# Block-diagonal inverses, 64-row update steps and a hold on small steps in a delta-rule recurrence with a gated MLP

## The chip, the cores and the metric

The kernel runs on one core of a Trainium2 chip. A core has a tensor engine (PE, with a sequencer of its own for weight loads, PEld in the profile), a vector engine (VectorE, DVE), a scalar engine (ScalarE, ACT), GpSimd (POOL) and SyncE (SP), which starts most transfers. The metric is the device time of one execution in microseconds (us). Before the change the median of three runs is 633.71 us (633.09 to 634.2).

## The reference

```python
# q, k, v: (B, H, S, D) = (4, 8, 768, 48); beta: (4, 8, 768); all f32
k_n = k / (norm(k, axis=-1) + 1e-06)
state = zeros((B, H, D, D))
for t in range(S):
    y[:, :, t] = einsum('bhd,bhde->bhe', q[:, :, t], state)
    v_old = einsum('bhde,bhd->bhe', state, k_n[:, :, t])
    state += beta[:, :, t, None, None] * einsum('bhd,bhe->bhde', k_n[:, :, t], v[:, :, t] - v_old)
x = y.transpose(0, 2, 1, 3).reshape(3072, 384)
out = (sigmoid(x @ w_gate) * (x @ w_val)) @ w_out      # w_gate, w_val 384 x 1536, w_out 1536 x 384
```

So 32 independent recurrences (4 batches by 8 heads) of 768 tokens each, and a gated MLP on the result.

## The kernel before

**Groups.** The 768 tokens are cut into 12 groups g of 64 tokens. Inside a group the recurrence is solved in closed form for all 32 heads together. The Gram matrix of the keys gives a lower triangular 64x64 system for each head, cut into two halves of 32 tokens: two 32x32 diagonal blocks and a 32x32 corner under them. VectorE inverts the diagonal blocks, for two groups (a pair) at once, one row of the solution after the other; the transposed inverses of a pair lie in `mt`. Tiles have 128 partitions, four quarters of 32: a head's 64 tokens fill one half of the partitions, and of the 32 heads half lie in partitions 0-63 and half in 64-127. `e` says whether a head's two token halves stand in order (0) or swapped (1), `x` in which half of the partitions (together with e) they stand, `j` counts the 8 heads of each of the four kinds (e, x).

**The steps of a group on PE**, each of many small f32 matmuls on parts of the 128x128 array, four in turn on different parts: `pg` (Gram, `gram`, L254); `pp` (keys by queries, `masked`, L273, then masked on VectorE); `pk` (keys by state, `rest`, L384); the first solution `pu` (step 0 of `updates`, L414, inverse by R = v - pk); its product with the corner (step 1, L407, added into pk); the second solution (step 2, L414 again); `yy` (outputs, `rows`, L442 and L445); `pd` (the change of the state, `advance`, L469); and the transposes `pt` (`flip`, L500), which give the x of the MLP. Between them VectorE subtracts (`less`, L393) and updates the state `su` (L478), and ScalarE copies solutions out of PSUM (`keep_u`, L422) and outputs (`keep_y`). Groups 0 and 1 start the program: they invert only 16x16 blocks and join them by two products, `pz` and `pm` (`joining`, L366), which `lower_left` feeds.

**The MLP.** Groups 0 and 1 form a unit each (tiles 256 tokens wide), then two groups a unit (512 wide). A gate or value tile (`gate_val`, L521, lines `gv_g` and `gv_v`) has 9 matmuls, 3 slices of the model's width by 3 products of values split into two parts; an output tile (`outp`, L557, `po`) has 9 too. Before the first gate tile PE fills gaps with dummy matmuls, `warm` (L185).

**The order.** `schedule()` plans every engine's order when the program is built: each step is a task with a cost in ns, what it comes after and which buffers it takes and frees (`pools`); a table `URGENCY` shifts tasks. Engines then run their queues in that fixed order, with semaphores between them. Transfers go through SyncE's queue: per group `dk` and `dq` (keys and queries by dimension, into `kqp`), `dv` (v and beta) and `dt` (k rows, for pd).

## Time and profile before

| what | value |
|---|---|
| median of 3 runs | 633.71 us (633.09 to 634.2) |
| the profiled execution | 636.26 us, of it 634.5 us span of the core |
| mean TensorE clock granted | 0.991 |
| PE busy | 617.0 us, 97% of the span, 9372 records |
| weight loads (PEld) | 502.4 us, 79% |
| VectorE | 393.7 us, 62% |
| ScalarE | 255.9 us, 40% |
| GpSimd | 10.0 us, 2% |
| largest groups | po 167.5, gv_g 167.3, gv_v 136.9 us on PE |

In a row of a group stand line, engine, operation, out<-in, for PE rows the place on the array (rows*columns) and the moving operand, the number of records, then busy us and mean ns of one, then the idle time before it and what ended most of it. In a row of stretches stand the stretch, its length, and the busy time (records) of PE, PEld, DVE, ACT and POOL, the granted clock, the share of the DMA engines and GB/s. In a row of the timeline stand start and length in us, and records in a run of like instructions. A row of waits has the waiting group, the releaser, then us in all, how often, and the longest.

### The profile page before, as it was taken

The numbers are of one execution on the slowest core, as the hardware profiler recorded it, in microseconds if no ns is written. First come the engines' busy times: TensorE is split into PE (matmuls) and PEld (weight loads), VectorE is DVE, ScalarE is ACT, GpSimd is POOL, SyncE is SP. The second block draws the span as 40 slices with busy tenths as digits, with TensorE's granted clock in tenths as the row PEclk, the third lists the DMA queues.
The fourth block names the chain that finished last, engine by engine and source line by source line (L and its number), as shares of the span: only waits on it lengthen the run. The fifth ranks groups of instructions, "written<-read, shape, count | busy, mean of one in ns | idle before, by whom it ended". The sixth has DMA issues, their size and how long they took to land.

```text
span 634.5 us, 20716 instructions
## 1 busy us (share of the span) xinstructions
PE 617.0 (97%) x9372; PEld 502.4 (79%) x9381; DVE 393.7 (62%) x876; ACT 255.9 (40%) x506; POOL 10.0 (2%) x25
## 2 busy tenths in 40 slices
PE   8878999999999999999999999999999999999997
...
GB/s 220 263 167 219 190 189 96 2 28 113 61 50 26 27 110 38 2 74 5 23 112 28 35 101 2 26 66 48 35 101 1 1 3 3 2 51 0 1 1 50
DMA packets 16216, 40.75 MB, mean 64 GB/s; under 512 B 2944, under 2 KB 3968, under 8 KB 16128
## 3 DMA queue, kind: packets, MB, share of 16 engines
...
## 4 chain that ended last, share of the span: by engine, by line
PE 87%; ACT 5%; DVE 5%; issue 1%; DMA 1%; SPq 0%; ACTq 0%
PE gv_g L521 26%; PE po L557 22%; PE gv_v L521 20%; PE pu L414 3%; PE warm L185 3%; PE pk L384 2%; PE pp L273 2%; PE yy L442 2%; PE pg L254 2%; PE yy L445 2%; ACT G L258 1%; PE pd L469 1%; PE pt L500 1%; PE pk L407 1%; ACT w L172 1%
## 5 line engine op out<-in xcount | busy, mean ns | idle before, releaser
L521 PE MATMUL gv_g<-x,w 128*128 128x512 f32 (+1 forms) x756 | 167.3, 368 | 0.7 <-DVE x L509 0.6
L557 PE MATMUL po<-h,w 128*128 128x512 f32 (+1 forms) x756 | 167.5, 366 | 0.3 <-DVE h L541 0.2
L557 PEld LDWEIGHTS po<-h,w 128*128 128x128 f32 x756 | 127.1, 188 | 25.1 <-DVE h L541 0.7
L521 PEld LDWEIGHTS gv_g<-x,w 128*128 128x128 f32 x756 | 126.7, 190 | 24.8 <-DVE x L509 0.9
L521 PE MATMUL gv_v<-x,w 128*128 128x512 f32 x540 | 136.9, 397 | 0.0
L521 PEld LDWEIGHTS gv_v<-x,w 128*128 128x128 f32 x540 | 99.9, 188 | 23.4
L536 ACT CAST h<-sg 128x512 fp32r<-128x512 f32 (+1 forms) x84 | 47.0, 559 | 144.0 <-DVE sg L531 139.7
L531 DVE TENSOR_TENSOR sg<-sg,gv_v 128x512 f32<-128x512 f32 x60 | 41.2, 687 | 97.9 <-PE gv_v L521 97.5
L526 ACT ACTIVATE sg<-gv_g 128x512 f32<-128x512 f32 (+1 forms) x84 | 45.0, 536 | 123.7 <-PE gv_g L521 123.4
L541 DVE TENSOR_TENSOR h<-sg,h 128x512 fp32r<-128x512 f32 (+1 forms) x84 | 51.4, 611 | 44.4 <-ACT h L536 43.9
L422 ACT COPY su<-pu 32x384 f32<-32x384 f32 x92 | 43.3, 470 | 51.8 <-PE pu L414 50.5
L305 DVE TENSOR_TENSOR tmp<-X,gp 128x31 f32<-128x31 f32 (+15 forms) x155 | 52.9, 341 | 4.1
L308 DVE TENSOR_TENSOR X<-X,tmp 128x31 f32<-128x31 f32 (+15 forms) x155 | 52.9, 342 | 3.8
L278 DVE TENSOR_TENSOR kqp<-pp,pmask 64x512 f32<-64x512 f32 x48 | 32.3, 686 | 7.6 <-PE pp L273 7.0
L478 DVE TENSOR_TENSOR su<-su,pd 48x384 f32<-48x384 f32 x40 | 22.0, 551 | 20.3 <-PE pd L469 19.6
L258 ACT COPY G<-pg 32x256 f32<-32x256 f32 (+1 forms) x66 | 26.0, 393 | 10.9 <-PE pg L254 9.5
L521 PE MATMUL gv_g<-xx,w 128*128 128x256 f32 x216 | 28.3, 285 | 0.7 <-DVE sg L531 0.7
L521 PEld LDWEIGHTS gv_g<-xx,w 128*128 128x128 f32 x216 | 26.6, 191 | 1.2 <-DVE sg L531 0.9
L185 PE MATMUL warm<-zero 128*128 128x512 bf16 x83 | 23.2, 430 | 2.4 <-issue 1.3
L393 DVE TENSOR_TENSOR R<-v,pk 128x384 f32<-128x384 f32 x44 | 22.3, 550 | 4.7 <-PE pk L384 4.2
L509 DVE TENSOR_TENSOR x<-pt,x 128x384 fp32r<-128x384 f32 x22 | 11.7, 554 | 19.9 <-ACT x L507 19.8
L414 PEld LDWEIGHTS pu<-R,mt 32*32 32x32 f32 x1408 | 16.6, 105 | 6.2 <-issue 5.1
...
## 6 DMA issues: line engine op xcount, KB each, us to landing
...
```

The source lines that it names most:

```text
L185: nc.tensor.matmul(out=hot[0], lhsT=z.to_broadcast([128, 128]), rhs=z.to_broadcast([128, 512]), start=True, stop=True)
L258: (nc.vector.tensor_copy if g < 2 and e else nc.scalar.copy)(out=G[lo:hi, :, e * J:(e + 1) * J], in_=pg[e][lo:hi, :, o:o + 32].rearrange(" ...
L305: nc.vector.tensor_tensor(out=tmp, in0=X[:, j:32, j:j + 1].to_broadcast([128, n, j]), in1=gp[:, j:j + 1, 0:j].to_broadcast([128, n, j]), o ...
L308: nc.vector.tensor_tensor(out=X[:, j:32, 0:j], in0=X[:, j:32, 0:j], in1=tmp, op=ALU.add)
L414: nc.tensor.matmul(out=pu[0 if g else x][r:r + 32, j], lhsT=mt[r:r + 32, g % 2, e * J + j], rhs=R[e][r:r + 32, j], start=True, stop=True)
L422: nc.scalar.copy(su[r:r + 32, 3 if x else e], pu[0][r:r + 32])
L521: nc.tensor.matmul(out=pg, lhsT=parts[w, f][:, a, k * 128:(k + 1) * 128], rhs=x[b][:, k], start=(k == 0 and q == 0), stop=(k == KC - 1 and ...
L526: nc.scalar.activation(h, st["g", f], AF.Sigmoid)
L531: nc.vector.tensor_tensor(out=h, in0=h, in1=st["v", f], op=ALU.mult)
L536: nc.scalar.copy(hh[:, 0], st["sg", f])
L541: nc.vector.tensor_tensor(out=hh[:, 1], in0=st["sg", f], in1=hh[:, 0].bitcast(F32), op=ALU.subtract)
L557: nc.tensor.matmul(out=po[k], lhsT=parts["o", f][:, w, k * 128:(k + 1) * 128], rhs=hh[:, a], start=begins(p, f) and q == 0 and (p > 1 or k ...
```

## The change

- **Wide updates.** From group 2 on (`WIDE`) `both` holds, for each head pair j, a 64x64 block diagonal of two 32x32 inverses: heads in the odd quarters are laid out swapped by the host (`v_rows`, `bt`), `aside` (ScalarE) copies the odd quarters' inverses to the right half of the columns, and `blank` (GpSimd) clears the left. `updates` then has 16 matmuls of 64 rows and 64 columns for a solution in place of 32 of 32 by 32. For all groups `across` (`pl`, L459 of the new kernel) does the corner product with 16 such matmuls from `uc`, a ScalarE copy of the whole first solution (`keep_all`), and `corner_of`, which holds two corners in a 64x64 block. Since partitions now meet other tiles of pk, `less` takes pk in quarters, directly or by four copies `pc` (`gather`), and `less_first` subtracts pl. The subtraction is done in place in v; R goes, and so does pk of group 0 (the state is zero there).
- **Joining product.** `pz` has 32 matmuls of 64 rows instead of 64 of 32; `lower_left` runs in four quarters. `pm` stays.
- **Planner.** New costs and a new `URGENCY`; a cost of 180 for the first small step behind an MLP tile in place of a rebate of 200 for the following ones; `HOLDS`: behind an MLP tile a small step of the groups from 4 on is taken only if it has been ready for so long (pp 25000 ns, pt 1000). `SHIFTS` 2 for 5. The k rows have one buffer for two, so dt of a group waits for pd of the one before.

The core of the diff:

```diff
-    mt = const.tile([128, 2, CP, 32], F32, name="mt")
+    both = const.tile([128, 2, 2, J, 2, 32], F32, name="both")
+    flat = both.rearrange("p g s j h i -> p (g s j h i)")
+    mt = flat[:, 0:2 * CP * 32].rearrange("p (g c i) -> p g c i", g=2, c=CP)
+    corner_of = [const.tile([128, J, 2, 32], F32, name=f"L{i}") for i in range(2)]
...
-    scratch = wk.tile([128, 3, CP, 32], F32, name="scratch", tag="xa0", bufs=1)
+    scratch = wk.tile([128, 1536], F32, name="scratch", tag="xa0", bufs=1)
+    wide_a = scratch[:, 0:1024].rearrange("p (c h i) -> p c h i", c=CP, h=2)
+    turned = scratch[:, 1024:1536].rearrange("p (c i) -> p c i", c=CP)
...
-        st["kv"[part]] = wk.tile([128, CP, D], F32, name=f"{'kv'[part]}_{g}", tag="kv"[part], bufs=2)
+        st["kv"[part]] = wk.tile([128, CP, D], F32, name=f"{'kv'[part]}_{g}", tag="kv"[part], bufs=part + 1)
...
-        st["L"] = L = wk.tile([128, CP, 32], F32, name=f"L_{g}", tag="L", bufs=2)
+        L = corner_of[g % 2]
...
+            to = (1 - e if n and g >= WIDE else e) * J
+            (nc.vector.tensor_copy if g < 2 and e else nc.scalar.copy)(out=G[lo:hi, :, to:to + J], in_=pg[e][lo:hi, :, o:o + 32].rearrange("q p t -> q t p"))
...
-            nc.scalar.copy(L[lo:lo + 32, e * J:(e + 1) * J], pg[e][lo:lo + 32, :, o:o + 32])
+            nc.scalar.copy(L[lo:lo + 32, :, 1 - e], pg[e][lo:lo + 32, :, o:o + 32])
...
-        nc.vector.transpose(mt.rearrange("q g c i -> q i c g"), X.rearrange("q i (c g) -> q i c g", g=2))
-        yield
-    def lower_left(g):
-        a = scratch[:, 0]
-        nc.scalar.activation(a[:, :, 0:16].rearrange("q c t -> q t c"), state[0]["G"][:, 0:16, :, g], AF.Copy, scale=under)
+        to = both[:, :, :, :, 0].rearrange("q g s j i -> q i (s j) g") if g >= WIDE else mt.rearrange("q g c i -> q i c g")
+        nc.vector.transpose(to, X.rearrange("q i (c g) -> q i c g", g=2))
+        yield
+    def aside(q):
+        nc.scalar.copy(both[32 * q:32 * q + 32, :, :, :, 1], both[32 * q:32 * q + 32, :, :, :, 0])
+    def blank(q):
+        nc.gpsimd.memset(both[32 * q:32 * q + 32, :, :, :, 0], 0.0)
+    def emptied(g):
+        nc.gpsimd.memset(flat[:, 1024 * g:1024 * g + 1024], 0.0)
+    def lower_left(g, q):
+        mine = slice(32 * q, 32 * q + 32)
+        nc.scalar.activation(wide_a[mine, :, q % 2, 0:16].rearrange("q c t -> q t c"), state[0]["G"][mine, 0:16, :, g], AF.Copy, scale=under[mine])
...
-        lhsT, rhs = (scratch[:, 0], mt[:, g]) if n == "pz" else (scratch[:, 1], scratch[:, 2])
-        out, rhs = out[:, :, 16:], rhs[:, :, 16:]
+        out = out[:, :, 16:]
         for c in range(CP):
-            for r in range(0, 128, 32):
-                last = nc.tensor.matmul(out=out[r:r + 32, c], lhsT=lhsT[r:r + 32, c], rhs=rhs[r:r + 32, c], start=True, stop=True)
+            if n == "pz":
+                for r in (0, 64):
+                    last = nc.tensor.matmul(out=out[r:r + 64, c], lhsT=wide_a[r:r + 64, c], rhs=mt[r:r + 64, g, c, 16:], start=True, stop=True)
+            else:
+                for r in range(0, 128, 32):
+                    last = nc.tensor.matmul(out=out[r:r + 32, c], lhsT=turned[r:r + 32, c], rhs=state[0]["z"][r:r + 32, c], start=True, stop=True)
...
+                nc.tensor.matmul(out=pk[e][t:t + 64, j], lhsT=kq[r:r + D, x, j], rhs=su[r:r + D, 2 if x else e, j], start=True, stop=True)
+    def halves_of(g):
+        return state[g]["v"].rearrange("p (s j) d -> p s j d", s=2)
+    def gather(g, q):
+        st, rows = state[g], slice(32 * q, 32 * q + 32)
+        if q == 0:
+            st["pc"] = wk.tile([128, J, D], F32, name=f"pc_{g}", tag="uc", bufs=2)
+        nc.scalar.copy(st["pc"][rows], st["pk"][1 ^ q % 2][rows])
+    def less(g, s, q=None):
+        rows = slice(0, 128) if q is None else slice(32 * q, 32 * q + 32)
+        r, st = halves_of(g)[rows, s], state[g]
+        nc.vector.tensor_tensor(out=r, in0=r, in1=st["pk"][s] if g < WIDE else st["pc"] if q is None else st["pk"][s ^ q % 2][rows], op=ALU.subtract)
+    def less_first(g, s):
+        r = halves_of(g)[:, s]
+        nc.vector.tensor_tensor(out=r, in0=r, in1=state[g]["pl"], op=ALU.subtract)
+    def updates(g, s):
+        st, R = state[g], halves_of(g)
+        st["pu", s] = pu = [ps_aux.tile([128, J, D], F32, name=f"pu_{g}_{s}_{x}", tag="aux") for x in range(1 if g or not s else 2)]
+        for j in range(J):
+            if g >= WIDE:
+                for r in (0, 64):
+                    nc.tensor.matmul(out=pu[0][r:r + 64, j], lhsT=both[r:r + 64, g % 2, s, j], rhs=R[r:r + 64, s, j], start=True, stop=True)
+                continue
+            for e, x in KINDS:
+                r = tokens_at(e, x) + 32 * (s ^ e)
+                nc.tensor.matmul(out=pu[x % len(pu)][r:r + 32, j], lhsT=mt[r:r + 32, g % 2, e * J + j], rhs=R[r:r + 32, e, j], start=True, stop=True)
+    def keep_all(g):
+        state[g]["uc"] = uc = wk.tile([128, J, D], F32, name=f"uc_{g}", tag="uc", bufs=2)
+        nc.scalar.copy(uc, state[g]["pu", 0][0])
+    def across(g):
         st = state[g]
+        st["pl"] = pl = ps_aux.tile([128, J, D], F32, name=f"pl_{g}", tag="aux")
         for j in range(J):
+            for r in (0, 64):
+                nc.tensor.matmul(out=pl[r:r + 64, j], lhsT=corner_of[g % 2][r:r + 64, j], rhs=st["uc"][r:r + 64, j], start=True, stop=True)
+    def keep_u(g, s, e, x):
+        r, pu = tokens_at(e, x) + 32 * (s ^ e), state[g]["pu", s]
+        (nc.vector.tensor_copy if g == 0 and x else nc.scalar.copy)(out=su[r:r + 32, 3 if x else e], in_=pu[x % len(pu)][r:r + 32])
...
-            transfer(f"dv{g}", lambda: load_rows(g, 1), 2 - g % 2, 1350 - g % 2 * 200, has(f"pd{g - 2}", f"less{g - 2}.1.1"), take=("flight",))
+            transfer(f"dv{g}", lambda: load_rows(g, 1), 2 - g % 2, 1350 - g % 2 * 200, has(f"pd{g - 2}"), take=("flight",))
         if what == "t":
-            transfer(f"dt{g}", lambda: load_rows(g, 0), 1, 1150, has(f"pd{g - 2}", *[QUIET] * (g == 1)), take=("flight",))
+            transfer(f"dt{g}", lambda: load_rows(g, 0), 1, 1150, has(f"pd{g - 1}", *[QUIET] * (g == 1)), take=("flight",))
...
+        blanks[g] = []
+        for q in (1, 3):
+            task(f"E{g}.{q}", ACT, 1050, lambda q=q: aside(q), [f"T{g}"])
+            blanks[g].append(task(f"F{g}.{q}", POOL, 1000, lambda q=q: blank(q), [f"E{g}.{q}"]))
...
-        task(f"ll{g}", ACT, 750, lambda g=g: lower_left(g), [f"G{g}.{e}.2" for e in range(2)], take=("scratch",), free=("G",) if g else ())
+        for q in range(4):
+            task(f"ll{g}.{q}", ACT, 750, lambda q=q: lower_left(g, q), [f"G{g}.{e}.2" for e in range(2)] + has(f"ll{g}.{q - 1}"), take=("scratch",) * (q == 0), free=("G",) if g and q == 3 else ())
...
-        task(f"pz{g}", PE, 1500, lambda g=g: joining(g, "pz"), ["mt0", f"ll{g}"] + has(LATER) + has("shift0")[:1 - g], take=(bank,))
+        task(f"pz{g}", PE, 1075, lambda g=g: joining(g, "pz"), ["mt0"] + [f"ll{g}.{q}" for q in range(4)] + has(LATER) + has("shift0")[:1 - g], take=(bank,))
...
-        task(f"pk{g}", PE, 970, lambda: rest(g), [f"dk{g}"] + was + has(f"h{g}.50", f"gram{g + 1}"), take=("aux", "aux"))
-        task(f"pp{g}", PE, 1130, lambda: pp.__setitem__(g, masked(g)), [f"dk{g}", f"dq{g}"] + (has(f"pt{g - 1}.1") if g < 3 else has(f"u{g - 1}.1")), take=(bank, bank))
+        if g:
+            task(f"pk{g}", PE, 1079, lambda: rest(g), [f"dk{g}"] + was + has(f"h{g}.50", f"gram{g + 1}"), take=("aux", "aux"))
+        task(f"pp{g}", PE, 1092, lambda: pp.__setitem__(g, masked(g)), [f"dk{g}", f"dq{g}"] + (has(f"pt{g - 1}.1") if g < 3 else has(f"a{g - 1}")), take=(bank, bank))
...
+                r = [task(f"less{g}.0.{q}", DVE, 555, lambda q=q: less(g, 0, q), [f"pk{g}", scaled] + has(f"less{g}.0.{q - 1}")) for q in range(4)]
+                for q in range(4):
+                    task(f"pc{g}.{q}", ACT, 472, lambda q=q: gather(g, q), r[-1:] + has(f"pc{g}.{q - 1}"), take=("uc",) * (q == 0), free=("aux", "aux") if q == 3 else ())
+                r.append(task(f"less{g}.1", DVE, 520, lambda: less(g, 1), [f"pc{g}.3", scaled], free=("uc",)))
...
+        word, pay = ("U", 600) if g >= WIDE else ("u", 812)
+        task(f"{word}{g}.0", PE, pay, lambda: updates(g, 0), r[:4] + ([f"T{g if g < 2 else g - g % 2}"] if g < WIDE else blanks[g - g % 2]), take=("aux",))
+        task(f"uc{g}", ACT, 472, lambda: keep_all(g), [f"{word}{g}.0"], take=("uc",))
+        k0 = keeps(0, [f"{word}{g}.0", f"uc{g}"])
+        task(f"a{g}", PE, 600, lambda: across(g), [f"uc{g}"] + corners[g], take=("aux",), free=("L", "uc"))
+        kind = (1,) if g >= WIDE else (0, 1)
+        l2 = [task(f"less{g}.2.{k}", DVE, 555, lambda k=k: less_first(g, k), [f"a{g}"] + r, free=("aux",) if k else ()) for k in kind]
+        task(f"{word}{g}.2", PE, pay, lambda: updates(g, 1), l2, take=("aux",) * (2 if two else 1), free=("mt",))
+        k2 = keeps(1, [f"{word}{g}.2"])
...
+                if e == PE and not shape[0] and not filling:
+                    options = [o for o in options if o[0] >= when[o[1]["n"]] + HOLDS.get(o[1]["name"].rstrip("0123456789."), 0) or int(o[1]["name"].strip("abcdefghijklmnopqrstuvwxyzU").split(".")[0]) < 4] or options
+                    soon = min(a for a, _ in options)
...
-                cost -= TURNED if small and shape[0] else 0
+                cost += SWITCH if small and not shape[0] and not filling else 0
...
-    TURNED = 200
+    SWITCH = 180
+    HOLDS = dict(gram=0, pp=25000, pt=1000, pk=0, pd=0)
...
+    other = np.arange(CP) ^ J
+    k_rows, v_rows = (by_token(x).reshape(N, 4, 32, CP, D) for x in (k, v))
+    v_rows[WIDE:, 1::2] = v_rows[WIDE:, 1::2][:, :, :, other]
+    kv_of = [x.reshape(N, 128, CP * D) for x in (k_rows, v_rows)]
+    bt = by_token(beta).reshape(N, 2, 2, 32, CP)
+    bt[WIDE:, :, 1] = bt[WIDE:, :, 1][..., other]
+    bt = bt.transpose(1, 2, 4, 0, 3).reshape(NQ, N // 2, 2, 32)```

In the orders below a row is a line, an operation, out<-in by name and buffer number, the moving or the copied shape, what it waits for, and xN for N alike. gv_2_6 is a gate or value tile of the third unit (groups 2 and 3), feature block 6; pu_4 belongs to group 4.

PE at the first solution of group 4, before (the 32 matmuls of the step alternate between R_4_0 and R_4_1; the first six are shown):

```order
L521 MATMUL gv_2_6_v_3602<-x0_2_2732,w_9_1244 128x512
L414 MATMUL pu_4_0_0_3612<-R_4_0_3571,mt_75 32x48 [waits DVE_49,PE_49]
L414 MATMUL pu_4_0_0_3612<-R_4_1_3575,mt_75 32x48
L414 MATMUL pu_4_0_0_3612<-R_4_0_3571,mt_75 32x48
L414 MATMUL pu_4_0_0_3612<-R_4_1_3575,mt_75 32x48
L414 MATMUL pu_4_0_0_3612<-R_4_0_3571,mt_75 32x48
L414 MATMUL pu_4_0_0_3612<-R_4_1_3575,mt_75 32x48
```

The same place on PE now:

```order
L563 MATMUL gv_2_6_v_3397<-x0_2_2615,w_9_1182 128x512
L442 MATMUL pu_4_0_0_3414<-v_4_2569,both_75 64x48 [waits DMAHW1_49,DVE_49,Pool_49]
L442 MATMUL pu_4_0_0_3414<-v_4_2569,both_75 64x48 [waits DVE_49,Pool_49]
L442 MATMUL pu_4_0_0_3414<-v_4_2569,both_75 64x48 x14
L599 MATMUL po_2_0_0_3078<-h_2_5_3378,w_8_891 128x512 [waits Activation_49]
L599 MATMUL po_2_0_0_3078<-h_2_5_3378,w_8_891 128x512 x2
L599 MATMUL po_2_0_1_3079<-h_2_5_3378,w_8_891 128x512 x3
L599 MATMUL po_2_0_2_3080<-h_2_5_3378,w_8_891 128x512 x3
L459 MATMUL pl_4_3448<-uc_4_3443,L0_76 64x48 [waits Activation_49]
L459 MATMUL pl_4_3448<-uc_4_3443,L0_76 64x48 x15
L284 MATMUL pp_5_0_3468<-kqp1_74 64x64 [waits DMAHW1_49]
```

The step stands behind the same tile with half the matmuls, the corner product one output tile later, and pp of the next group follows it in the same run of small steps.

ScalarE from that solution to the second one of group 4, before:

```order
L422 COPY su_76<-pu_4_0_0_3612 32x384 [waits PE_49]
L422 COPY su_76<-pu_4_0_0_3612 32x384 x3
L536 CAST h_2_6_3660<-sg_2_6_3592 128x512 [waits DVE_49]
L526 ACTIVATE sg_2_7_3694<-gv_2_7_g_3646 128x512 [waits PE_49,Activation_49]
L422 COPY su_76<-pu_4_2_0_3709 32x384 [waits PE_49]
L422 COPY su_76<-pu_4_2_0_3709 32x384 x3
```

And now:

```order
L422 COPY pc_4_3410<-pk_4_1_3345 32x384 [waits DVE_49]
L422 COPY pc_4_3410<-pk_4_0_3344 32x384
L422 COPY pc_4_3410<-pk_4_1_3345 32x384
L422 COPY pc_4_3410<-pk_4_0_3344 32x384
L451 COPY uc_4_3443<-pu_4_0_0_3414 128x384 [waits PE_49]
L464 COPY su_78<-pu_4_0_0_3414 32x384 x4
L578 CAST h_2_6_3466<-sg_2_6_3407 128x512 [waits DVE_49]
L464 COPY su_78<-pu_4_1_0_3504 32x384 [waits PE_49]
L464 COPY su_78<-pu_4_1_0_3504 32x384 x3
```

Four copies of pk and one of the whole solution come in; the copies into the state tile stay.

PE ahead of the first MLP tile, now (before, pz_1 has 64 matmuls of form 32x16 there, from mt and scratch):

```order
L195 LDWEIGHTS zero_82
L195 MATMUL warm_113<-zero_82 128x512
L390 MATMUL pz_1_792<-both_75,scratch_84 64x16 [waits DVE_49]
L390 MATMUL pz_1_792<-both_75,scratch_84 64x16 x31
L563 MATMUL gv_0_0_g_830<-x0_0_765,w_0_618 128x256 [waits Activation_49]
```

The place is the same; the number of matmuls is halved.

More of the change, by code (lines that the diff above doesn't have):

```diff
@@ L383, in rest @@
                 r, t = 64 * e, tokens_at(e, x)
-                nc.tensor.matmul(out=pk[e][t:t + 64, j], lhsT=kq[r:r + D, x, j], rhs=su[r:r + D, 2 if x else e, j],
-                                 start=j == 0, stop=True, skip_group_check=True)
-        if g:
-            st["R"] = [None, None]
-    def less(g, e, step):
-        st = state[g]
-        if st["R"][e] is None:
-            st["R"][e] = wk.tile([128, J, D], F32, name=f"R_{g}_{e}", tag="row", bufs=2)
-        nc.vector.tensor_tensor(out=st["R"][e], in0=st["v"][:, e * J:(e + 1) * J], in1=st["pk"][e], op=ALU.subtract)
@@ L395, in updates @@
-    def updates(g, step):
-        st = state[g]
-        if g == 0 and "R" not in st:
-            st["R"] = [st["v"][:, e * J:(e + 1) * J] for e in range(2)]
-        R, L = st["R"], st["L"]
-        at = {(e, x): [tokens_at(e, x) + 32 * (k ^ e) for k in range(2)] for e, x in KINDS}
-        if step == 1:
-            for j in range(J):
-                for e, x in KINDS:
-                    one, two = at[e, x]
-                    nc.tensor.matmul(out=st["pk"][e][two:two + 32, j], lhsT=L[one:one + 32, e * J + j], rhs=su[one:one + 32, 3 if x else e, j],
-                                     start=False, stop=True, skip_group_check=True)
-            return
-        st["pu"] = pu = [ps_aux.tile([128, J, D], F32, name=f"pu_{g}_{step}_{x}", tag="aux") for x in range(1 if g else 2)]
-        for j in range(J):
-            for e, x in KINDS:
-                r = at[e, x][step // 2]
-                nc.tensor.matmul(out=pu[0 if g else x][r:r + 32, j], lhsT=mt[r:r + 32, g % 2, e * J + j], rhs=R[e][r:r + 32, j], start=True, stop=True)
@@ L684, in pair @@
         by_name[h[-1]]["free"] = ("gp",)
-        task(f"T{g}", DVE, 1990, lambda: next(gen), [h[-1]], take=("mt", "mt"), free=("G",))
+        if g < WIDE:
+            task(f"T{g}", DVE, 1990, lambda: next(gen), [h[-1]], take=("mt", "mt"), free=("G",))
+            return
+        if g == WIDE:
+            for i in range(2):
+                task(f"Z{i}", POOL, 1000, lambda i=i: emptied(i), [f"u{g - 1}.2"])
+        task(f"T{g}", DVE, 1990, lambda: next(gen), [h[-1]] + has("Z0", "Z1")[:2 if g == WIDE else 0], take=("mt", "mt"), free=("G",))
+        blanks[g] = []
+        for q in (1, 3):
+            task(f"E{g}.{q}", ACT, 1050, lambda q=q: aside(q), [f"T{g}"])
+            blanks[g].append(task(f"F{g}.{q}", POOL, 1000, lambda q=q: blank(q), [f"E{g}.{q}"]))
     def halves():
@@ L735, in recurrence, with keeps @@
         kinds = [(e, x) for e, x in KINDS]
         two = g == 0
-        def keeps(step, before):
-            out = []
+        def keeps(k, before):
+            out, split = [], two and k
             for i, (e, x) in enumerate(kinds):
-                f = ("aux",) if (two and i >= 2) or i == 3 else ()
-                if two:
-                    f = ("aux",) if i % 2 else ()
+                f = ("aux",) if i == 3 or split and i == 1 else ()
                 eng = DVE if two and x else ACT
-                out.append(task(f"u{g}.{step}.{i}", eng, 560 if eng == DVE else 472, lambda e=e, x=x: keep_u(g, step, e, x), before + has(f"yy{g - 1}", f"pd{g - 1}"), free=f))
+                out.append(task(f"u{g}.{2 * k}.{i}", eng, 560 if eng == DVE else 472, lambda e=e, x=x: keep_u(g, k, e, x), before + has(f"yy{g - 1}", f"pd{g - 1}", *out[-1:] if not split or i % 2 else ()), free=f))
@@ L746, in keeps @@
             return out
-        task(f"u{g}.0", PE, 810, lambda: updates(g, 0), r + [f"T{g if g < 2 else g - g % 2}"], take=("aux",) * (2 if two else 1))
-        k0 = keeps(0, [f"u{g}.0"])
-        task(f"u{g}.1", PE, 810, lambda: updates(g, 1), k0 + corners[g] + r, free=("L",))
-        l1 = [task(f"less{g}.1.{e}", DVE, 555, lambda e=e: less(g, e, 1), [f"u{g}.1"], free=("aux",)) for e in range(2)]
-        task(f"u{g}.2", PE, 810, lambda: updates(g, 2), l1, take=("aux",) * (2 if two else 1), free=("row", "row", "mt") if g else ("mt",))
@@ L791, in out_of @@
         wide = len(UNITS[p]) > 1
[L792 removed]
+        task(f"out{i}", PE, 2100 if wide else 1070, lambda: outp(p, f), [f"hl{i}", f"wlo{number[f // 2 * 2, 'oo']}"] + has(f"out{i - 1}") + (cleared if begins(p, f) else []), take=("po", "po") + ("aux",) * wide if begins(p, f) else (), free=("h",))
         if ends(p, f):
```

77 lines of the change are left out of this document (38 added, 39 removed), and 13 rows, old and new, of the table URGENCY.

## The prediction

> **What bounds the kernel now.** I read the head of the page first, then the busy time by stretches, then TensorE's timeline in one pair of groups.
>
> ```profile
> span 634.5 us, 20716 instructions
> PE 617.0 (97%) x9372; PEld 502.4 (79%) x9381; DVE 393.7 (62%) x876; ACT 255.9 (40%) x506; POOL 10.0 (2%) x25
> PE 87%; ACT 5%; DVE 5%; issue 1%; DMA 1%; SPq 0%; ACTq 0%
> 50.62:171.85 121.23, 115.56 (x2500) 109.59 (x2492) 96.30 (x215) 77.88 (x165) 1.91 (x2) 0.99 0.39 111
> 171.85:545.00 373.15, 373.15 (x5460) 297.53 (x5461) 240.01 (x544) 128.34 (x258) 2.91 (x3) 1.00 0.14 39
> ...
> 542.00 0.82 PE L500 MATMUL pt<-ident,ys 128*128 128x128 f32 x6
> ```
>
> TensorE (PE) is busy 617.0 of 634.5 us and carries 87% of the chain that ended last. The two lines of the stretches (length, then PE, weight loads, VectorE, ScalarE, GpSimd) say where: from the first tile of the gated MLP at 50.62 to 171.85 PE stands idle for 5.7 us in all; from 171.85 to 545.00 not at all, and the last row, of the timeline, shows the last small step begin at 542.00. So in that stage every us of PE work added or saved moves the end by as much, and what the other engines do there is hidden.
>
> Now one group of the recurrence. The numbers in front are start and length; the length includes a modelled tail, so I price a step by its start to the next start.
>
> ```profile
> 202.18 2.26 PE L521 MATMUL gv_g<-x,w 128*128 128x512 f32 x9
> 204.28 2.26 PE L521 MATMUL gv_v<-x,w 128*128 128x512 f32 x9
> 222.32 0.88 PE L414 MATMUL pu<-R,mt 32*32 32x48 f32 x64
> 223.14 1.19 PE L273 MATMUL pp<-kqp 48*64 48x64 f32 x64
> 224.25 2.37 PE L557 MATMUL po<-h,w 128*128 128x512 f32 x9
> 226.55 1.15 PE L442 MATMUL yy<-su,kqp 48*64 48x48 f32 x64
> 227.63 1.14 PE L445 MATMUL yy<-su,kqp 128*64 128x48 f32 x32
> 228.70 2.36 PE L521 MATMUL gv_g<-x,w 128*128 128x512 f32 x9
> 230.99 0.94 PE L469 MATMUL pd<-su,k 64*48 64x48 f32 x64
> 231.86 0.55 PE L500 MATMUL pt<-ident,ys 128*128 128x128 f32 x3
> ...
> 241.20 0.88 PE L407 MATMUL pk<-su,L 32*32 32x48 f32 x64
> 242.01 2.35 PE L521 MATMUL gv_v<-x,w 128*128 128x512 f32 x9
> ```
>
> Every f32 matmul of the recurrence leaves two records, so x64 is 32 matmuls. A 32-row step (pu, or pk of L407) takes 0.81 to 0.82 us (I use 0.81), pd 0.87, pp 1.11, the yy of L442 1.08 and that of L445 1.07 with half the records. Counting by places on the array (a place is the rows times the columns that one matmul covers): L442 and pp cycle through four places of 64 columns, pd through four of 48, pu through four of 32, L445 through two of 64 columns that are 128 rows high. In every one of these steps a place gets 16 records. So a place turns a record around in 1.07/16 = 67 ns with 64 columns, whether two or four places share the array, in 54 ns with 48 and in 51 ns with 32.
>
> A 9-record tile takes 2.10 us among its like (202.18 to 204.28) and 2.30 between two small steps (224.25 to 226.55): a run of small steps costs 0.2 us for the two changes, however many steps stand in it.
>
> **The change, part by part.**
>
> *The update steps.* In groups 2 to 11 each of the three steps (first solution, its product with the corner, second solution) now has 16 matmuls of 64 rows by 64 columns in place of 32 of 32 by 32; in groups 0 and 1 only the product with the corner has. Those are 30 + 1 steps behind the first MLP tile and one ahead of it. A wide step uses two places, rows 0-63 to columns 0-63 and rows 64-127 to columns 64-127. Its 32 records are again 16 for each place. The nearest row is L445: two places, 64 columns, 48 moving columns, 32 records, 1.07 us; only the rows differ, and the 48-row L442 shows the same 67 ns. I take 1.07. That is 0.26 more than the 0.81 of now: half the matmuls, but as many per place, and each place turns slower because it has 64 columns to load. 31 x 0.26 = **+8.1 us**. The lower end is half of a four-place step of 64 records, 1.08/2 = 0.54, that is 31 x -0.27 = -8.4; the upper end is pp's 1.11, +9.3.
>
> The weight loads speak for the columns as the cause:
>
> ```profile
> L414 PEld LDWEIGHTS pu<-R,mt 32*32 32x32 f32 x1408 | 16.6, 105 | 6.2 <-issue 5.1 <-ACT L L262 0.4
> L469 PEld LDWEIGHTS pd<-su,k 64*48 64x48 f32 x704 | 9.0, 121 | 3.4 <-issue 2.9 <-PE yy L445 0.3
> L442 PEld LDWEIGHTS yy<-su,kqp 64*64 64x64 f32 x384 | 10.1, 134 | 0.7 <-DVE su L420 0.4 <-issue 0.3
> L445 PEld LDWEIGHTS yy<-su,kqp 128*64 128x64 f32 x384 | 12.2, 138 | 0.7
> ```
>
> 105, 121, 134 and 138 ns for 32, 48, 64 and 64 columns: a load grows by about 0.9 ns a column and hardly with the rows or with the number of places.
>
> In a wide step both places write one PSUM bank. The two 32-row steps above differ in just that: pu writes one bank from four places, pk of L407 two banks, and both take 0.81 us, so I give this no price. The Trainium skill (TensorEngine Tiling, Gotcha 1: PSUM Pressure) says that different row tiles cannot access one bank at the same time; by it the 32 records would go one after the other, 32 x 67 ns = 2.1 us a step and some +41 us in all. The trace does not agree: pu does it four-fold without loss.
>
> *The joining product pz.* 32 matmuls of 64 rows instead of 64 of 32 rows, for groups 0 and 1.
>
> ```profile
> 27.98 1.26 PE L366 MATMUL pz<-mt,scratch 32*32 32x16 f32 x128
> 49.43 1.26 PE L366 MATMUL pz<-mt,scratch 32*32 32x16 f32 x128
> 50.62 2.37 PE L521 MATMUL gv_g<-x,w 128*128 128x256 f32 x18
> ```
>
> Now 1.19 us, 32 records for each of four places, 37 ns each with 16 moving columns. Then 32 records for each of two places, at up to 67 ns 2.1 us, or as the other end at 34 ns 1.1. Group 1's stands right ahead of the first MLP tile: +0.9. Group 0's lies in the first group's chain, but a wait of PE follows it (the 1.8 us below) which may take it in: half, +0.45. Ends for both: -0.2 to +1.9.
>
> *The first group's chain.* Between its first and second solution stood two copies one after the other on each engine, 32 matmuls and two subtractions; now one ScalarE copy of all 128 rows, 16 wide matmuls and the two subtractions.
>
> ```profile
> 37.45 1.14 DVE L420 COPY su<-pu 32x384 f32<-32x384 f32 x2 [1.07 <-PE pu L414]
> 38.69 1.09 PE L407 MATMUL pk<-su,L 32*32 32x48 f32 x64
> L422 ACT COPY su<-pu 32x384 f32<-32x384 f32 x92 | 43.3, 470 | 51.8 <-PE pu L414 50.5
> L393 DVE TENSOR_TENSOR R<-v,pk 128x384 f32<-128x384 f32 x44 | 22.3, 550 | 4.7 <-PE pk L384 4.2 <-PE pk L407 0.3
> ```
>
> 1.14 becomes 0.47 (-0.67); the product 1.09 becomes 1.09 x 67/51 = 1.43 (+0.34): -0.3. The zero product pk of group 0 goes; the dummy matmuls (warm) that follow it are its cover, so nothing.
>
> *Fewer runs of small steps.* In the orders of instructions the runs between MLP tiles are 78 now and 74 then: -4 x 0.2 = -0.8. The hold on the pairs' small steps gives no more than this, as they keep nearly as many runs.
>
> *Instruction waits.* While the weights come in, PE waits five times for nothing that the profile shows:
>
> ```profile
> PE pz L366 <- issue: 1.8, 1, 1.8
> PE pm L366 <- issue: 1.3, 1, 1.3
> PE pg L254 <- issue: 1.2, 1, 1.2
> PE pu L414 <- issue: 0.9, 1, 0.9
> PE pk L384 <- issue: 0.8, 1, 0.8
> 0.00:30.00 30.00, 26.93 (x456) 15.31 (x460) 20.14 (x64) 13.99 (x26) 5.18 (x20) 1.00 0.87 245
> 30.00:60.00 30.00, 22.63 (x818) 18.02 (x826) 24.23 (x34) 23.28 (x37) 0.00 (x0) 0.88 0.66 188
> 60.00:90.00 30.00, 28.08 (x650) 26.66 (x643) 22.85 (x40) 26.62 (x51) 0.96 (x1) 0.95 0.67 187
> ```
>
> 6.0 us over 1924 matmul records. The change takes 256 of them out there (64 of pk, 32 of each corner product, 64 of each pz), 13%: -0.8, with +2 and -4 as ends, since a moved wait may meet other work.
>
> *What I cost at nothing.* Three more rows, of the waits and of the groups:
>
> ```profile
> PE gv_g L521 <- DVE x L509: 0.6, 1, 0.6
> ...
> L316 ACT ACTIVATE scratch<-G,under 128x256 f32<-128x256 f32 x2 | 1.5, 758 | 0.3 <-DVE G L258 0.3
> L577 ACT COPY ot<-po 128x512 f32<-128x512 f32 x14 | 8.1, 586 | 2.1 <-PE po L557 1.4
> ```
>
> ScalarE gets per group from 2 on four quarter copies of pk and one of the first solution (5 x 0.47), per pair two copies of a quarter of the inverse (about 1 us each, an estimate: twice a 512-element copy), and six more mask products of 0.76 for groups 0 and 1: some 39 us. VectorE gets two subtractions more a group (six for four, 32 rows costing what 128 do): 11 us. In the stage without PE idle they have 245 and 133 us free; were that cover gone, the x of a pair would come late and its first gate tile wait, as it now does once for 0.6 us. GpSimd's ten quarter clears stand before a pair's first solution only, on an idle engine. From 60 to 90 ScalarE has 3.4 us free and gets only group 1's copy there, 0.5. On the queue of SyncE the k rows now have one buffer, so each such transfer waits for pd of the group before, and what is behind it too; it is needed only by its own group's pd, most of a group's chain later.
>
> Sum: 8.1 + 0.9 + 0.45 - 0.3 - 0.8 - 0.8 = +7.5 us. The profiled execution took 636.26 (634.5 and 1.76 around it), 2.55 above the median of 633.71; I add the sum to the median: **641.2 us**.
>
> **Rivals.**
>
> *Half the matmuls, half the time (faster).* If the rows' halves were what is shared, each half would give a record every 34 ns (pp, L442 and L445 fit this too), and a wide step, 16 records to a half, would take 0.54: -8.4. With pz -0.2, the chain -0.8 and the last two terms -1.6 it ends at 622.7. Against it: pu and pz differ by 32 moving columns, and per half this would be 25 less 19 ns, 0.2 ns a column, while an MLP tile streams 512 columns in 2.10/9 = 233 ns, 0.46 a column. Per place it is 51 less 37 ns, 0.44 a column, which fits. It decides from a wide step under 0.76 us on. The Trainium skill (TensorEngine Tiling, Instruction Overhead) counts about 60 cycles for every matmul however narrow; by that count too the step would halve. The trace gives 32 records of L445 the time of 64 of L442.
>
> *No change in the steps.* If only the loads of places in one half queue up, a half with one place is free of it, and the 51 ns of streaming 48 columns stay: 0.81 a step, as now. Then pz -0.1, the chain -0.6, runs -0.8, waits -0.8: 631.4. For it speaks that streaming set the pace in pu; against it that the load's length grows with columns in the same way where nothing shares.
>
> *The order comes apart early.* Steps that take longer than the planner's table gives them come late between 50 and 172, where 5.7 us idle already stand: +2 to +5 on top of the first case, its upper part.
>
> **How the numbers follow.** Wide steps as L445: 0.62, own range 637 to 646 (the ends of the instruction waits, and +5). Steps unchanged: 0.18, half of it faster, a third within the bound. Half time: 0.20. The range 624 to 646 leaves out most of the last case and a little above. Within 0.2% (1.3 us), about what a measurement can tell here, ends 0.07; faster 0.31; slower 0.62.
>
> **What would show it.** Groups of form 64*64 64x48 for pu and pl; from such a step's start to the next start 1.07 (rivals 0.81, 0.54); pz of group 1 near 2.1 where now 1.19; 74 runs; still no PE idle after the pairs begin; PE's busy time up by some 8 us. Wrong it would be if two places turned faster than 51 ns.

## The result and the profile after

The changed kernel takes 641.76 us (median of 4 runs, 640.4 to 643.45) where the kernel before took 633.85: ratio 1.0128, 95% interval 1.0098 to 1.0157. Beside the first experiments it took 641.0 where the one before took 634.52: 1.0113 (1.0087 to 1.014). So it is 6.5 to 7.9 us slower; 641.2 was forecast. Its profiled execution took 640.40 us. The head of its page and the stretches:

```profile
span 638.6 us, 18434 instructions
PE 620.1 (97%) x8160; PEld 507.6 (79%) x8167; DVE 405.4 (63%) x896; ACT 291.3 (46%) x574; POOL 22.7 (4%) x39
...
50.62:171.85 121.23, 114.17 (x2188) 108.69 (x2189) 103.15 (x236) 83.41 (x178) 5.66 (x6) 0.97 0.37 103
171.85:545.00 373.15, 373.15 (x4677) 299.95 (x4676) 245.16 (x543) 153.18 (x305) 10.46 (x11) 1.00 0.14 40
```

PE has 1212 records fewer and is still full from 171.85 to 545.00, while ScalarE does 25 us more there than before: its copies are hidden, as costed. TensorE's timeline in one group:

```profile
213.46 1.13 PE L442 MATMUL pu<-v,both 64*64 64x48 f32 x32
214.53 2.35 PE L599 MATMUL po<-h,w 128*128 128x512 f32 x9
216.81 0.96 PE L459 MATMUL pl<-uc,L 64*64 64x48 f32 x26
217.56 0.27 PE L284 MATMUL pp<-kqp 48*64 48x64 f32 x2
...
217.73 1.16 PE L284 MATMUL pp<-kqp 48*64 48x64 f32 x59
218.72 1.09 PE L442 MATMUL pu<-v,both 64*64 64x48 f32 x32
219.74 2.35 PE L563 MATMUL gv_g<-x,w 128*128 128x512 f32 x9
```

Between two tiles a wide step takes 213.46 to 214.53 = 1.07 us, the price that was forecast. But pl, with pp behind it, has only 26 of its records out when pp starts 0.75 us after it; the two then run mixed. A wide step uses two places; the places of pp on the other halves are free and need not wait.

Three profiles of the kernel before and two of the changed one (before_a, before_b and again are from the experiments), each cut at the first MLP tile and at the last matmul's end:

| profile | time | start to first tile | to last matmul | behind it |
|---|---|---|---|---|
| before | 636.26 | 50.62 | 580.34 | 3.54 |
| before_a | 635.52 | 50.56 | 579.68 | 3.56 |
| before_b | 634.73 | 51.09 | 578.34 | 3.57 |
| after | 640.40 | 47.13 | 586.91 | 4.56 |
| again | 640.73 | 50.11 | 584.36 | 4.43 |

In the mean the start is 2.1 shorter, the MLP 6.2 longer and the tail 0.9 longer, +5.0; the profiled executions lie in the mean below their medians (after) and above (before), which makes the rest.

How the +5.0 falls on start and MLP depends on the clock too. In these five profiles TensorE's granted clock drops to 0.50 for stretches of 3.4, 6.8 or 10.2 us, not at the same place in each. The stretches ahead of the first tile and around it, of before_a, after and again:

```profile
28.00:44.00 16.00, 11.38 (x365) 6.77 (x365) 12.68 (x19) 9.86 (x16) 0.00 (x0) 0.68 0.72 208
44.00:72.00 28.00, 24.89 (x796) 22.21 (x788) 22.61 (x35) 24.34 (x42) 0.00 (x0) 1.00 0.67 192
28.00:44.00 16.00, 12.68 (x440) 9.17 (x444) 14.80 (x22) 15.16 (x24) 0.00 (x0) 1.00 0.72 207
44.00:72.00 28.00, 23.41 (x658) 21.67 (x657) 22.74 (x34) 24.26 (x42) 1.85 (x2) 0.88 0.75 204
28.00:44.00 16.00, 13.04 (x399) 8.77 (x399) 11.60 (x18) 11.93 (x18) 0.00 (x0) 0.79 0.70 217
44.00:72.00 28.00, 24.49 (x691) 22.31 (x690) 25.44 (x38) 27.24 (x47) 1.85 (x2) 0.94 0.72 209
```

The loss is a stretch's length times what its clock lacks to 1: in before_a 16 x 0.32 = 5.1 us in the first stretch and none in the second, in after none and 28 x 0.12 = 3.4, in again 3.4 and 1.7. In the mean the three profiles before lose 4.5 us in the first stretch and 0.6 in the second, the two of the changed kernel 1.7 and 2.6. So up to 2.8 us of the shorter start and up to 2.0 of the longer MLP may be the place where the half clock fell: these are upper ends, since a loss counts only where TensorE is what the rest waits for. The sums of both stretches are alike (5.1 and 4.3), so the clock does not make the slowdown as a whole. Why the stretches fall where they do was not tried.

### The profile page after: what moved, and what is told of

It reads as the page before. It is cut to its first block, busy times and chain, and to the rows that moved or that the text cites. A ratio compares the mean times of both kernels' runs of the same rounds, so it can differ in the third digit from the quotient of the medians.

```text
span 638.6 us, 18434 instructions
## 1 busy us (share of the span) xinstructions
PE 620.1 (97%) x8160; PEld 507.6 (79%) x8167; DVE 405.4 (63%) x896; ACT 291.3 (46%) x574; POOL 22.7 (4%) x39
## 4 chain that ended last, share of the span: by engine, by line
PE 84%; DVE 7%; ACT 4%; DMA 2%; issue 2%; SPq 0%; ACTq 0%; DVEq 0%
PE gv_g L563 23%; PE po L599 21%; PE gv_v L563 20%; PE pu L442 3%; PE warm L195 2%; PE pp L284 2%; PE pl L459 2%; PE yy L484 2%; PE yy L487 2%; DMA raw<-in_words_dram 2%; PE pg L264 2%; PE pk L411 2%; DVE X L319 1%; DVE tmp L316 1%; PE pd L511 1%
## 5 line engine op out<-in xcount | busy, mean ns | idle before, releaser
L563 PE MATMUL gv_g<-x,w 128*128 128x512 f32 (+1 forms) x756 | 167.2, 368 | 0.4 <-DVE sg L573 0.2
L599 PE MATMUL po<-h,w 128*128 128x512 f32 (+1 forms) x756 | 167.0, 365 | 0.1
L563 PEld LDWEIGHTS gv_g<-x,w 128*128 128x128 f32 x756 | 127.1, 191 | 24.8 <-DVE sg L573 0.7
L599 PEld LDWEIGHTS po<-h,w 128*128 128x128 f32 x756 | 126.9, 188 | 24.6 <-DVE h L583 0.6
L563 PE MATMUL gv_v<-x,w 128*128 128x512 f32 x540 | 137.1, 398 | 0.0
L563 PEld LDWEIGHTS gv_v<-x,w 128*128 128x128 f32 x540 | 99.7, 188 | 23.7 <-DVE sg L573 0.5
L578 ACT CAST h<-sg 128x512 fp32r<-128x512 f32 (+1 forms) x84 | 46.9, 559 | 140.1 <-DVE sg L573 139.2
L573 DVE TENSOR_TENSOR sg<-sg,gv_v 128x512 f32<-128x512 f32 x60 | 41.2, 686 | 95.4 <-PE gv_v L563 94.8
L583 DVE TENSOR_TENSOR h<-sg,h 128x512 fp32r<-128x512 f32 (+1 forms) x84 | 51.4, 613 | 24.3 <-ACT h L578 23.9
L464 ACT COPY su<-pu 32x384 f32<-32x384 f32 x92 | 43.3, 470 | 12.3 <-PE pu L442 11.2
L520 DVE TENSOR_TENSOR su<-su,pd 48x384 f32<-48x384 f32 x40 | 22.0, 551 | 12.5 <-PE pd L511 11.9
L563 PE MATMUL gv_g<-xx,w 128*128 128x256 f32 x216 | 28.4, 285 | 1.6 <-DVE sg L573 1.6
L563 PEld LDWEIGHTS gv_g<-xx,w 128*128 128x128 f32 x216 | 26.6, 191 | 2.1 <-DVE sg L573 1.8
L269 ACT COPY G<-pg 32x256 f32<-32x256 f32 (+1 forms) x66 | 23.0, 392 | 10.1 <-PE pg L264 9.5
L551 DVE TENSOR_TENSOR x<-pt,x 128x384 fp32r<-128x384 f32 x22 | 11.8, 552 | 24.3 <-ACT x L549 24.0
L195 PE MATMUL warm<-zero 128*128 128x512 bf16 x90 | 23.7, 412 | 2.1 <-issue 1.1
L428 DVE TENSOR_TENSOR v<-v,pk 32x384 f32<-32x384 f32 (+1 forms) x42 | 23.0, 549 | 3.8 <-PE pk L411 3.2
L422 ACT COPY pc<-pk 32x384 f32<-32x384 f32 x40 | 18.8, 470 | 12.1 <-DVE v L428 11.6
## 6 DMA issues: line engine op xcount, KB each, us to landing
out_dram<-ot SPq DMA_DIRECT2D x7, 128.0 KB, 1.9
```

The lines of the kernel that those rows point to most:

```text
L195: nc.tensor.matmul(out=hot[0], lhsT=z.to_broadcast([128, 128]), rhs=z.to_broadcast([128, 512]), start=True, stop=True)
L269: (nc.vector.tensor_copy if g < 2 and e else nc.scalar.copy)(out=G[lo:hi, :, to:to + J], in_=pg[e][lo:hi, :, o:o + 32].rearrange("q p t -> ...
L464: (nc.vector.tensor_copy if g == 0 and x else nc.scalar.copy)(out=su[r:r + 32, 3 if x else e], in_=pu[x % len(pu)][r:r + 32])
L563: nc.tensor.matmul(out=pg, lhsT=parts[w, f][:, a, k * 128:(k + 1) * 128], rhs=x[b][:, k], start=(k == 0 and q == 0), stop=(k == KC - 1 and ...
L573: nc.vector.tensor_tensor(out=h, in0=h, in1=st["v", f], op=ALU.mult)
L578: nc.scalar.copy(hh[:, 0], st["sg", f])
```

## The experiments

All medians are beside runs of the kernel before on the same chip: 634.52 us for the first four, 635.15 for n32z and cost, 634.82 for bwide and bhold.

**The changed kernel again.** No edit.

> The changed kernel unaltered, for a second profile and times on the same chip as the other runs. Expected: 640.4 to 643.5 us, as in its four runs. If the first MLP tile starts near 47 us again (47.13 in the first profile, 50.62 in that of the kernel before), the start has really become shorter; if it starts near 50, the first profile was a short one and the sum of the prediction is met by other terms.

641.0 us (639.85 to 642.62). Its first tile starts at 50.11, so 47.13 was an early start; 3 us of spread between executions of one program lie there. The half clock goes with it: ahead of the tile again loses 3.4 us to it, after nothing.

**The form of the wide steps.** Two edits, the same results by other matmuls; n32:

```diff
-                for r in (0, 64):
-                    nc.tensor.matmul(out=pu[0][r:r + 64, j], lhsT=both[r:r + 64, g % 2, s, j], rhs=R[r:r + 64, s, j], ...)
+                for q in range(4):
+                    r = 32 * q
+                    nc.tensor.matmul(out=pu[0][r:r + 32, j], lhsT=both[r:r + 32, g % 2, s, j, q % 2], rhs=R[r:r + 32, s, j], ...)
```

and c6432, with the 64 rows kept and the columns halved:

```diff
...
+                for q in range(4):
+                    r, o = 64 * (q // 2), 32 * q
+                    nc.tensor.matmul(out=pu[0][o:o + 32, j], lhsT=both[r:r + 64, g % 2, s, j, q % 2], rhs=R[r:r + 64, s, j], ...)
```

and likewise for `across`.

> The changed kernel with the update steps of groups 2 to 11 and all corner products issued as 32 matmuls of 32x32 in place of 16 of 64x64; order, copies and every other instruction as in the changed kernel. Theory columns (a place with 64 columns takes 67 ns a record, one with 32 columns 51 ns): each of 31 steps from 1.00-1.07 back to 0.81 us, 6 to 8 us less than the changed kernel, so 634 to 636 us. Rival schedule (the loss lies in the new order, the copies and the waits): 641 to 643 us, and the doubled number of instructions might add to it.

> The same steps as 32 matmuls of 64 rows by 32 columns (each block column of the 64x64 block by itself, on four places: two row halves by two column quarters of each). Everything else as in the changed kernel. Theory columns: a place of 32 columns turns a record in 51 ns however high it is, a step takes 0.81 us, the time is that of the 32x32 form, 634 to 636 us. Rival rows (64 rows, or a row half being passed one record after the other, set the pace): 32 records a half at 33 ns give 1.07 us a step, so 641 to 643 us; if two matmuls on the same rows cannot overlap at all, 32 x 67 ns = 2.1 us a step and some 675 us.

n32: 638.93 us, ratio 1.0074 (1.005 to 1.0098). c6432: 638.27, 1.0069 (1.0042 to 1.0095). The timeline of c6432, at the place shown above:

```profile
213.50 0.88 PE L443 MATMUL pu<-v,both 64*32 64x48 f32 x64
214.31 2.37 PE L601 MATMUL po<-h,w 128*128 128x512 f32 x9
216.62 0.88 PE L461 MATMUL pl<-uc,L 64*32 64x48 f32 x64
217.43 1.16 PE L284 MATMUL pp<-kqp 48*64 48x64 f32 x64
218.52 0.79 PE L443 MATMUL pu<-v,both 64*32 64x48 f32 x52
220.13 0.36 PE L443 MATMUL pu<-v,both 64*32 64x48 f32 x12 [0.83 <-issue]
```

0.81 us a step with 64 rows and 32 columns on four places, exactly as with 32 rows: the columns set the pace, not the rows and not the number of matmuls, and the rival rows falls. The loads say the same: 107 ns for 64 rows by 32 columns (pu of c6432), 105 for 32 by 32 (n32), 135 for 64 by 64 (after).

The total gained only 2.1 and 2.7 us, not 6 to 8. The steps did give 5.2 and 5.5 (added up over the timeline from start to next start, without waits: the 31 wide steps of again take 31.0 us, those of n32 25.8, of c6432 25.5). Part of what is missing lies in the waits behind the first tile; those of n32:

```profile
PE pp L284 <- issue: 3.1, 1, 3.1
PE pd L513 <- issue: 1.0, 1, 1.0
PE pu L443 <- issue: 1.0, 2, 0.9
```

That is 5.1 us of waits for nothing that the profile shows, and 3.8 in c6432, where again has 2.1 and after 2.7. Two of them, before pd near 148 us and before pu near 220 us (1.0 and 0.9 in n32, 0.8 and 0.8 in c6432), are in neither profile of the changed kernel. But ahead of the first tile n32 and c6432 wait only 0.4 where the changed kernel waits 2.8 and 3.1, so over the whole run the sums are 5.5 and 4.2 against 5.5 and 5.2: that twice the matmuls wait longer is not shown. The half clock takes part too: behind the first tile it costs n32 3.4 us and c6432 5.1, again 1.7 and after 3.4. How the missing 3 us divide stays open.

**The wide form alone, in the order of before.**

```diff
...
+        for j in range(J) if g > 1 else ():
+            for r in (0, 64):
+                nc.tensor.matmul(out=pu[0][r:r + 64, j], lhsT=mt[r:r + 64, g % 2, 2 * j:2 * j + 2], rhs=R[j % 2][r:r + 64, j], start=True, stop=True)
...
```

and the corner product likewise, but for its first four matmuls, which stay 32x32.

> The kernel before in its own order, with only the form of the update steps changed: in groups 2 to 11 each solution has 16 matmuls of 64x64 in place of 32 of 32x32, and in all groups the corner product has 14 of 64x64 and 4 of 32x32. The wide matmuls take their weights from the tile of inverses as it lies there, so the results are not the recurrence's; no other engine's work, order or wait is changed. Theory columns, with what the changed kernel's trace added to it (a wide step takes 1.07 us between two tiles, 0.25 more than now, but lets a small step behind it start after 0.75, 0.07 less): 25 such steps stand before a tile and 6 before a small step, 25 x 0.25 - 6 x 0.07 = +5.8, less up to 1 for the instruction waits of 250 matmuls fewer by 90 us: 639.5 to 641 us. Rival schedule (the changed kernel lost its time in its order and copies, and the wide form is worth no more than the 2 to 3 us that the 32x32 form gained there): 636.5 to 638 us. Rival of the prediction's lower end: 0.54 a step, 626 us.

639.87 us, 1.0089 (1.0062 to 1.0116): +5.05, inside what theory columns expected. First tile at 50.88, tail 3.6, as before: all of it lies between. One solution and one corner product:

```profile
214.14 1.14 PE L416 MATMUL pu<-R,mt 64*64 64x48 f32 x32
215.21 2.35 PE L527 MATMUL gv_g<-x,w 128*128 128x512 f32 x9
217.49 0.29 PE L406 MATMUL pk<-su,L 32*32 32x48 f32 x8
217.71 1.02 PE L410 MATMUL pk<-su,mt 64*64 64x48 f32 x28
218.66 2.35 PE L527 MATMUL gv_v<-x,w 128*128 128x512 f32 x9
```

That +5.05 fits so well is partly luck: the mixed corner product takes 1.17 us, 0.1 more than a pure wide step, and the 31 steps of bwide take 32.6 us where before has 25.5 in the mean, +7.1; some of that came back, since its waits for nothing that the profile shows are 2.0 us where before has 3.7 to 6.0. Still, without any change of order or copies, the form of the matmuls alone slows the kernel by an amount that makes most of the 6.5 to 7.9; everything else in the change adds up to some 1.5 to 3.

**The joining product back to 32 rows** (on top of n32).

```diff
-                for r in (0, 64):
-                    last = nc.tensor.matmul(out=out[r:r + 64, c], lhsT=wide_a[r:r + 64, c], rhs=mt[r:r + 64, g, c, 16:], ...)
+                for q in range(4):
+                    r = 32 * q
+                    last = nc.tensor.matmul(out=out[r:r + 32, c], lhsT=wide_a[r:r + 32, c, q % 2], rhs=mt[r:r + 32, g, c, 16:], ...)
```

> The 32x32 form of the update steps and corner products (as in the run n32: 638.9 us) and also the joining products of groups 0 and 1 as 64 matmuls of 32x32 in place of 32 of 64x64. Theory of the prediction: the one right ahead of the first MLP tile goes from 1.97 us back to 1.19 and that of group 0 by as much, the latter hidden in part: 0.8 to 1.6 us less than n32, 637.3 to 638.1 us. Rival (both hidden in a start that ends with something else, a transfer or an instruction wait): as n32, 638.9.

641.13 us, 1.0114 (1.0082 to 1.0146), where n32 had 1.0074 (1.005 to 1.0098): no gain; a loss is not shown, as the intervals overlap. In the profiled execution, a long one of 645.32 us, PE waits at the start for nothing that the profile shows:

```profile
PE pd L514 <- issue: 2.5, 1, 2.5
PE pz L394 <- issue: 2.3, 1, 2.3
PE pt L545 <- issue: 1.6, 1, 1.6
```

Ahead of the first tile these and a smaller one add up to 6.6 us, where n32 has 0.4. The wide pz does take 1.97 us where it stands, but the time that its 32-row form should have given back was not seen; whether the doubled matmuls made these waits, or the long execution, one profile cannot say. Both expectations missed the number.

**The hold.** nohold empties the changed kernel's table (`HOLDS = {}`); bhold adds the same lines to the planner of before.

> The changed kernel planned without the hold on small steps of the pairs (its table of holds empty). In the order of instructions 75 runs of small steps stand between MLP tiles where the changed kernel has 74. Theory of the prediction (a run costs 0.2 us, nothing else): +0.2 us, no measurable change, 641 to 643 us. Rival (the hold is what keeps the pairs in step or what makes x late): off by 2 us or more in one direction.

> The kernel before with only the hold on small steps of the pairs added to its planner (pp held 25000 ns, pt 1000, as in the change); 78 runs of small steps stay 78. Theory of the prediction (a run costs 0.2 us and the hold takes hardly one away): no measurable change, 634 to 636 us. Rival (the hold by itself saves what the changed kernel planned without it lost, 1 to 2 us): 632.5 to 634.

nohold: 643.05, 1.0145 (1.012 to 1.0171); bhold: 634.98, 1.0007 (0.9989 to 1.0025). In the order of before the hold changes nothing. Without it the changed kernel's interval still overlaps that with it, but its profile has a wait of PE in the stage of the pairs that the two of the changed kernel do not have:

```profile
304.65 1.90 PE L599 MATMUL po<-h,w 128*128 128x512 f32 x7 [1.19 <-DVE h L583]
```

**True prices in the planner.**

```diff
-        word, pay = ("U", 600) if g >= WIDE else ("u", 812)
+        word, pay = ("U", 1070) if g >= WIDE else ("u", 812)
-        task(f"a{g}", PE, 600, ...
+        task(f"a{g}", PE, 1070, ...
-        task(f"pz{g}", PE, 1075, ...
+        task(f"pz{g}", PE, 1970, ...
```

> The changed kernel planned with what its wide steps measured: 1070 ns for updates and corner products (the table had 600) and 1970 ns for the joining product (1075). The instructions are the same, their order is the planner's answer. Theory that the order came apart early because the table was wrong (VectorE's product of a tile stands behind too many rows of the inverse, PE waits 1.6 us for it near 112 us, and 0.6 us for a corner copy): these waits go and the time falls by 1 to 2.5 us, 639 to 640.5. Rival (PE is full from 172 us on, so the order matters only at the start, and there it is tuned by the table of urgencies that no longer fits): no gain, 641 to 643.

659.97 us, 1.0396 (1.0373 to 1.042), far outside both expectations. The waits and the first tile:

```profile
PE pt L542 <- ACT ys L502: 5.3, 1, 5.3
PE pk L411 <- DVE su L520: 4.0, 2, 3.7
...
63.64 3.62 PE L563 MATMUL gv_g<-x,w 128*128 128x256 f32 x18
```

With these prices and the old urgencies the planner puts pk, pm, pp and pu of group 1 ahead of the first tile, which starts at 63.64. Behind it PE waits 13.4 us in all, where again waits 4.7. Wrong prices do less harm here than right ones with an old table.

**The kernel before, two more profiles.** No edit.

> The kernel before, unaltered, for a second profile: its first one took 636.26 us where the median of 13 runs on the chip of the first experiments was 634.5. What is asked is the spread of the start: the first MLP tile began at 50.62 us in the first profile, with 6.0 us of waits of PE for nothing that the profile shows. If the first profile was a long one, this one starts its MLP 1 to 3 us earlier, near the 47 to 50 of the changed kernel's profiles, and the tail behind the last matmul shows whether its 3.54 us (4.2 to 4.6 in the changed kernel and its variants) is of this kernel or of that run.

> The kernel before once more, a third profile for the same question: 632 to 636 us, tail behind the last matmul 3.5 us if it belongs to the kernel, 4.2 to 4.6 if it belongs to the run.

635.52 and 634.73 us; first tile at 50.56 and 51.09, tails 3.56 and 3.57 (table above). The tail belongs to the kernel: 3.5 to 3.6 us in all five profiles with the order of before, 4.0 to 4.6 in all with the new one.

## Why the prediction was right, point by point

**Wide steps: the mechanism right, the sum too large.** The price from the nearest row (L445) was 1.07 us, and a wide step takes 1.07 between tiles; that columns set it is shown by c6432, and that it is the main loss by bwide. The mis-sized term is "31 x 0.26 = +8.1 us": the 31 steps behind the first tile take 31.0 us, the same 31 of before 25.5 (mean of the three profiles), so +5.5. Nine of them have another small step right behind them; where it is pp or pg, seven times, that one starts after 0.75, where it is pt, which takes the whole array, after 1.07. What failed in this term is to price every step alone and a run of steps by its ends only. The rivals' 0.81 and 0.54 are refuted by the rows. The Trainium skill's rule that different row tiles cannot access one bank at the same time (TensorEngine Tiling (Array Packing), Gotcha 1: PSUM Pressure) is again not borne out where the row tiles write different partitions: the wide steps write one bank from two row halves at the pace of L445.

**pz.** The row of group 1's:

```profile
45.16 2.04 PE L390 MATMUL pz<-both,scratch 64*64 64x16 f32 x64 [0.68 <-DVE x L551]
47.13 2.39 PE L563 MATMUL gv_g<-x,w 128*128 128x256 f32 x18
```

1.97 us for 2.1 forecast. From 1.07 for 16 records a place to 1.97 for 32 are 56 ns a record; if the moving columns (48 there, 16 here) make no difference, the 67 ns held 0.17 us of start and end per step. No run tried the two apart. That pz costs the whole +1.35 was not shown (n32z).

**The first chain: the -0.3 met in one pair of profiles, by luck.** The last part of the first solution and the start of the outputs, in after:

```profile
31.39 0.78 PE L446 MATMUL pu<-v,both 32*32 32x48 f32 x52 [0.91 <-issue]
...
37.60 0.89 PE L484 MATMUL yy<-su,kqp 64*64 64x48 f32 x32
```

From that part's end (32.17) to yy are 5.43 us; in the profile before, from 37.36 to 43.09, 5.73. But in before_a and before_b the same stretch takes 8.28 and 8.42, in again 6.89, so in the mean it is 1.3 shorter. The clock differs there: after ran it at 1.00, the others in part or wholly at 0.50.

**The start as a whole: not as forecast, the cause open.** The sum left the order of the start at nothing, and the clock. In the three profiles before, VectorE scales v between the two transposes of the inverses; now it does not:

```profile
25.60 1.04 DVE L342 STREAM_TRANSPOSE mt<-X 128x512 f32<-128x512 f32 x1
26.50 0.93 DVE L239 TENSOR_TENSOR v<-v,mq 128x768 f32<-128x768 f32 x1
27.35 1.03 DVE L342 STREAM_TRANSPOSE mt<-X 128x512 f32<-128x512 f32 x1
24.48 1.90 DVE L366 STREAM_TRANSPOSE both<-X 128x512 f32<-128x512 f32 x2
```

(three rows of before, one of after.) In the mean the first tile comes 2.1 us earlier, where the terms for pz gave +1.35 and the chain -0.3: the first solution ends 2.4 earlier, the chain is 1.3 shorter, and from the outputs to the tile it takes 1.6 longer, pz with its 0.8 among it. That this order is the cause was not tried by itself, and the place of the half clock is a rival: by the stretches above it can make up to 2.8 us of difference there.

**Instruction waits: wrong.** -0.8 was forecast; they add up to 6.0, 4.4 and 3.7 us in the profiles of before and to 5.5 and 5.2 now. The step that failed is to price them by the number of matmuls. Counting every instruction of TensorE in the trace, weight loads and the sequencer's own included, these waits stand at fixed places: in the ten profiles that lack no matmul record, each one of 0.16 us or more, but for one in n32z, has 961 instructions ahead of it or a multiple of 256 more, to within one. In again these are 961, 1473 and 2242, in n32 961, 2242, 5570 and 7873. How long PE waits there varies: 1.9 to 3.1 us behind the 2242 of again, nohold, n32 and c6432. In bwide, whose order is that of before, two of them are left, 2.0 us in all: that speaks for a gain from fewer matmuls, in one profile. The changed kernel and n32 (5.5 in all) do not show it.

**Runs of small steps: not seen.** 74 for 78, as forecast, but the MLP tiles take 470.7 and 470.8 us (start to next start) where the three profiles of before have 469.9 to 471.0. The half clock can hide 0.8 us here: before_a and before_b, without it behind the first tile, have 469.9 both, before, which loses 1.7 us there, 471.0.

**The order coming apart early: in part.** PE waits near 112 us for VectorE, whose product of a tile stands behind rows of the inverse:

```profile
113.68 2.41 PE L563 MATMUL gv_g<-xx,w 128*128 128x256 f32 x18 [1.64 <-DVE sg L573]
```

1.9 us with a smaller one, 0.7 before.

**Not forecast: the tail**, +0.9. The last store of after, of before:

```profile
634.99 0.38 ACTq L627 DMA_DIRECT2D out_dram<-ot  x1
out_dram<-ot ACTq DMA_DIRECT2D x1, 128.0 KB, 2.5
631.91 0.37 ACTq L585 DMA_DIRECT2D out_dram<-ot  x1
out_dram<-ot ACTq DMA_DIRECT2D x1, 128.0 KB, 1.7
```

Issue to landing takes 2.2 to 2.5 us in the changed kernel and its variants (nohold, n32, c6432, n32z, cost), 1.7 in the three profiles of before and in bwide and bhold. Why stays open.

**The signs.** The forms, 74 runs and no PE idle after the pairs begin came as said; PE's busy time rose by 3 to 6 us (620.1 and 622.8 against 616.7 to 617.0), not by some 8.

So the direction and the main cost were right by their mechanism, but that the total came within 1 us is luck, with errors on both sides: the steps 2.6 too dear and the start about 3 too late, against a tail, waits, the place of the half clock and a run-to-run part that were not in the sum.
